# First sums over the output weights, written into the ordered part of steps 18 to 21

## The chip, the cores and the metric

The kernel runs on one core of one Trainium2 chip. The metric is device microseconds of one execution; runs are compared by their medians. Three runs of the kernel before gave 511.87 us in the median (510.62 to 513.28).

## What is computed

Two stages in one program, both in 32-bit floats. The first is attention over 4 batches, 8 heads, 768 positions and 64 numbers a head. Every position sees its neighbours closer than 16, and 24 summaries of blocks of 32 positions (the largest key of a block, the mean of its values):

```python
scores_l_m = np.where(np.abs(pos[:, None] - pos[None, :]) < 16, scale * q @ k.T, -1e9)
scores_s = scale * q @ k_sum.T + np.log(32)
a = np.exp(scores_all - max)          # scores_all: both, side by side
a = a / (a.sum(-1) + 1e-9)
x = a @ concat(v, v_sum)              # heads side by side: 3072 x 512
```

The second is a network on those 3072 rows, with weights of 512x1024, 512x1024, 1024x1024 and 1024x512:

```python
h = ((x @ w1) * (x @ w2)) @ w3
out = h @ w_out
```

## The kernel before

**Precision.** TensorE multiplies a rounded 32-bit format here, so each operand is kept as a high part and a low part (`low`, line 120: the number less its rounded copy), and each product is three matmuls. ScalarE makes the rounded copy, VectorE the subtraction.

**Stages.** `w3` and `w_out` are first multiplied with each other into eight tiles `wp` (the output weights). The first 1024 rows go through the network in the plain way. The other 2048 rows, in two units n = 1 and 2, are multiplied by a scheme with seven products of half-size blocks in place of eight. It needs sums and differences of blocks: of the rows (`xT`, `moving_x`), of the gates' weights (`sums_of_gates`, stored to the device memory `wS`) and of the output weights (`sums_of_output`, stored to `pS`). `stationary` (line 665) makes such sums: four additions on VectorE (lines 689, 691, 695, 700) on the quarters `wr`, and for each result a cast on ScalarE (line 679, into a tile `sp`), the low half on VectorE (line 121), and a write by SyncE (line 685).

**The gates' products.** For a unit, `gates` runs twice (r = 0, 1) over seven products, and each over four banks of PSUM (tiles `ln`), with six matmuls of 512 columns a bank (line 740). After every product each bank is read out by `add_up`: a copy on ScalarE (line 758) or an addition on VectorE (line 760). The next product can't write a bank before. Each product takes two weight tiles `ws` of 512 KB, one for two banks. SyncE loads them (line 785) into six slots that they share with the tiles `sp` of the gates' sums.

**Attention beside it.** Steps 0 to 23 (a unit of 512 positions by a pair of heads) are interleaved with the network; from step 16 on two at a time, in `two_steps(m)` with steps 2m and 2m + 1. Each has scores (line 376), a masked minimum (line 390), exponentials (line 404), sums inverted (lines 409 and 410), a normalization (line 414), transposes (434, read out at 442 and 444) and products with the values (457, read out at 477). `PAIRS[0]` is 8.

**Order.** TensorE and GpSimd execute in the order in which the code was written. On ScalarE and VectorE the parts under `tc.manual_schedule(engines=VECTOR)` keep their order among themselves; all else is put by a scheduler where it sees room, and SyncE's queue is set by it too. Work in `background` is handed out one piece at a time by `tend` as TensorE's columns are written; once the order is set, each engine executes its own queue strictly one after the other.

**The sums of the output weights.** High and low part of `wp` are first added in device memory (`spill_high`, `join_wp`, into `pR`). `LATER` then calls `sums_of_output(0)` in the first half of m = 8 and `sums_of_output(1)` in that of m = 9. Each loads four pieces of 256 KB into `wr` (line 957) and puts `stationary(...)` into `background`.

Of the kernel before, what the change touches and what calls it, by code (L numbers as in the profile page):

```python
# [73 lines left out]
def attention_moe(ctx, tc, qG, kW, kT, vP, vW, vB, mask, w1, w2, w3T, wo, out, outT):  # L74
    nc = tc.nc
    B, NPAIR, _, S = kT.shape
# [13 lines left out]
    NF = w1.shape[0] * FQ // P  # L90
    NJ = w3T.shape[2] // 2 // P
    DO = out.shape[1]
    NK = 7
# [18 lines left out]
    wp = [sb.tile([P, 2, DO], F32R, name=f"wp{i}", tag="wp", bufs=NF) for i in range(NF)]  # L112
# [299 lines left out]
    def normalize(sm, mx):  # L412
        for j in range(NI):
            nc.scalar.activation(sm[:, j], sm[:, j], AF.Copy, scale=mx[:, 2, j : j + 1])  # L414
# [250 lines left out]
    def stationary(name, load, to_dram, home, apart=None):  # L665


        if apart is not None:
            t = apart
        else:  # L670
            whole = sb.tile([P, 2, 2, 512], F32, name="wr", tag="ring", bufs=RING)
            t = [[whole[:, i, j] for j in range(2)] for i in range(2)]
        yield from load(t)
        (a11, a12), (a21, a22) = t
        yield 1

        def finished(k, raw):
            to = sb.tile([P, 2, 512], F32R, name="sp", **home)
            nc.scalar.copy(to[:, 0], raw)
            yield 1  # L680
            low(nc.vector, to[:, 1], raw, to[:, 0])
            yield 1
            yield 1
            yield 1
            nc.sync.dma_start(to_dram(k), to.bitcast(F32))
            stored.add((name, k))

        works = []
        nc.vector.tensor_tensor(a22, a21, a22, ALU.add)
        yield 1  # L690
        nc.vector.tensor_tensor(a21, a11, a21, ALU.subtract)
        works.append(finished(2, a22))
        next(works[0])
        yield 1
        nc.vector.tensor_tensor(a11, a22, a11, ALU.subtract)
        works.append(finished(5, a21))
        next(works[0])
        next(works[1])
        yield 1
        nc.vector.tensor_tensor(a12, a12, a11, ALU.subtract)  # L700
        if apart is not None:
            yield from staggered([*works, finished(4, a11), finished(3, a12)])
            return

        yield from staggered(works)
        for _ in range(3):
            yield 1
        yield from staggered([finished(4, a11), finished(3, a12)])
# [57 lines left out]
    def moving_x(n, at):  # L766

        o = ORDERS[n]
        k = o.ids[at]

        def start():
            while any(kept.get((n, half), 0) < NC for half in range(2 if k > 1 else 1)):
                yield -1
            t = sb.tile([P, 2, KH, U], F32R, name="xT", tag="w12", bufs=8)
            works = []
            for c in range(KH):
                b = [[raws[n, half][c + i * KH] if (n, half) in raws else None for half in range(2)] for i in range(2)]
                works.append(moving(o, k, b, (t[:, 0, c], t[:, 1, c]), o.before.get(k, (k,))))
            yield from staggered(works)
            xT[n, k] = t  # L780

        tasks.append(start())
# [161 lines left out]

        return stationary("w%d" % q, load, lambda k: wS[k][q], {"tag": "x", "bufs": 6})

    def sums_of_output(c):

        if c:
            two = [sb.tile([P, 2, 512], F32, name="wr", tag="raw", bufs=2) for _ in range(2)]  # L950
            t = [[two[i][:, j] for j in range(2)] for i in range(2)]
        else:
            t = [[sb.tile([P, 512], F32, name="wr", tag="pt", bufs=4) for _ in range(2)] for _ in range(2)]
        for h in range(2):
            for i in range(2):
                to = t[i][h].rearrange("p (j d) -> p j d", d=DH)
                nc.sync.dma_start(to, pR[c][:, h, :, i * DH : (i + 1) * DH])
        background.append(stationary("p%d" % c, lambda _: range(1, 3), lambda k: pS[k][c], {"tag": "wp", "bufs": NF}, t))

    def network():  # L960
        for u in range(2):
# [299 lines left out]
    def begins(m):  # L1261
# [6 lines left out]
        15: [lambda: flow_in(4), lambda: moving_x(1, 2)],  # L1268
    }
    LATER = {  # L1270
        (PAIRS[0], 0): [lambda: sums_of_output(0)],
        (PAIRS[0], 1): [lambda k=k: moving_x(1, k) for k in range(3, NK)],
        (PAIRS[0] + 1, 0): [lambda: sums_of_output(1)],
    }

    for i in range(NF):
# [50 lines left out]
    def two_steps(m):  # L1327

        a, b = 2 * m, 2 * m + 1
        first = m == PAIRS[0]  # L1330
        if first:
            fetch_means(*place(a - 1), values[a - 1])
        with tc.manual_schedule(engines=VECTOR):
            if first:
                t, home = sms.pop(a - 2)
                pt = evacuate(transposes(t), "A", home)
            for p in (a - 4, b - 4):
                if p in turned:
                    finish_step(p, turned.pop(p), **SPARE)
            if m in PAIRS:  # L1340
                (u, sm, mx, sc), (u2, sm2, mx2, sc2) = [begin(p) for p in (a, b)]
                reduce(u, 0, sc, sm, mx)
                expose(0, sm, mx)
                reduce(u, 1, sc, sm, mx)
        if not first:
            fetch_values(a - 2)
        for work in LATER.get((m, 0), ()):
            work()
        if m in PAIRS:
            fetch(a + 2)  # L1350
            run(given[0] + LEAD / 2)
            with tc.manual_schedule(engines=VECTOR):
                expose(1, sm, mx)
                reduce(u2, 0, sc2, sm2, mx2)
                invert(mx)
            run(given[0] + LEAD / 2)
            with tc.manual_schedule(engines=VECTOR):
                if first:
                    finish_step(a - 2, pt, **SPARE)
                    turn((a - 1,), "A")  # L1360
                expose(0, sm2, mx2)
                reduce(u2, 1, sc2, sm2, mx2)
                normalize(sm, mx)
            if not first:
                fetch_values(b - 2)
            fetch(b + 2)
            run(CLASSIC + LAST_SINGLE * FAST if first else (given[0] + begins(m + 1)) / 2)
            with tc.manual_schedule(engines=VECTOR):
                if first:
                    finish_step(a - 1, turned.pop(a - 1), **SPARE)  # L1370
                expose(1, sm2, mx2)
                invert(mx2)
                normalize(sm2, mx2)
        if not first and m - 1 <= PAIRS[-1]:
            with tc.manual_schedule(engines=VECTOR):
                turn((a - 2, b - 2), "A")
        if m not in PAIRS:
            fetch_values(b - 2)
        for p in (a, b):
            fill(p + 2)  # L1380
            if not first and p - 2 in values:
                fetch_means(*place(p - 2), values[p - 2])
        for work in LATER.get((m, 1), ()):
            work()
        run(begins(m + 1))
# [75 lines left out]
```

## Time and profile before

| | |
|---|---|
| median of three runs | 511.87 us |
| the profiled execution | 513.02 us, of which the span is 511.2 |
| TensorE busy | 487.2 us (95%) |
| VectorE, ScalarE busy | 357.7 us (70%), 317.2 us (62%) |
| mean granted TensorE clock | 0.992 |
| moved by DMA | 139.29 MB, 272 GB/s in the mean |

The span runs from the first instruction to the last. Busy shares are means over stages that have different limits. A wait is read from the engine that waits; the idle time of an engine counts only where another engine waits for it in turn. The granted clock is 1.00 at the higher of TensorE's two levels and 0.50 at the lower.

### The profile page before, as it was taken

How to read it: one execution, taken by the hardware profiler on the slowest of the kernel's cores; microseconds unless marked ns; L12 is line 12 of the kernel's file. 1: busy time of each engine (PE TensorE's matmuls, PEld its weight loads, DVE VectorE, ACT ScalarE, POOL GpSimd, SP SyncE). 2: the span in 40 equal slices, each digit the busy share in tenths (PEclk: the TensorE clock that was granted, in tenths of full speed). 3: DMA queues.
4: the chain of work that ended last, by engine and by line, in shares of the span. 5: the costliest groups of instructions: out<-in, count | busy, mean ns of one | idle time of the engine just before them, and what ended most of it. 6: DMA issues, size and time to landing. Idle time of an engine off the chain costs nothing.

```text
span 511.2 us, 10548 instructions
## 1 busy us (share of the span) xinstructions
PE 487.2 (95%) x3804; PEld 393.5 (77%) x3804; DVE 357.7 (70%) x873; ACT 317.2 (62%) x882; POOL 61.3 (12%) x121
## 2 busy tenths in 40 slices
PE   0989999999999999999977999999999999999997
PEld 0767777888877878777856888888888888888886
DVE  5969886897703879875469787579969029229972
ACT  5589864776726978877974959579734421422710
POOL 1024522000212010000210304022000000000000
PEclk9999999999999999999997999999999999999999
DMA  8998697999599998888998989995859766656752
GB/s 341 413 410 272 223 361 252 364 402 388 161 324 242 287 260 284 281 293 287 336 296 288 309 313 317 368 259 181 233 187 248 254 190 199 197 178 204 211 188 96
DMA packets 56068, 139.29 MB, mean 272 GB/s; under 512 B 6224, under 2 KB 19280, under 8 KB 53456
## 3 DMA queue, kind: packets, MB, share of 16 engines
q1 hardware_dynamic: 51600, 127.44, 73.2%
q0 software_dynamic: 3264, 9.08, 7.7%
q10 hardware_dynamic: 1152, 2.10, 1.1%
q8 instruction: 30, 0.49, 0.4%
q14 instruction: 22, 0.18, 0.1%
HBM read 105.89 MB, written 32.70 MB: 271 GB/s over the span
## 4 chain that ended last, share of the span: by engine, by line
PE 76%; ACT 8%; DMA 7%; DVE 5%; issue 1%; POOL 0%; SPq 0%; POOLq 0%; DVEq 0%; ACTq 0%
PE ln L740 42%; PE mm L125 26%; PE po L457 4%; PE sc L376 3%; DMA k<-in_kW_dram 3%; PE tp L434 2%; DMA wr<-pR 2%; ACT wf L176 2%; ACT sm L404 2%; DVE wf L206 2%; ACT w L220 1%; DVE w L121 1%; DMA wraw<-in_w_dram 1%; DVE wf L203 1%; DMA wraw<-in_wo_dram 1%
## 5 line engine op out<-in xcount | busy, mean ns | idle before, releaser
L740 PE MATMUL ln<-xT,ws 128*128 128x512 f32 x672 | 158.8, 396 | 5.7 <-DVE tmp L760 4.9
L740 PEld LDWEIGHTS ln<-xT,ws 128*128 128x128 f32 x672 | 127.2, 191 | 34.3 <-DVE tmp L760 5.3
L125 PE MATMUL mm<-x,w 128*128 128x512 f32 x384 | 90.9, 394 | 0.5 <-DVE g L531 0.5
L125 PEld LDWEIGHTS mm<-x,w 128*128 128x128 f32 x384 | 71.1, 188 | 16.9 <-DVE g L531 0.9
L404 ACT ACTIVATE sm<-sm,mx 128x120 f32<-128x120 f32 x192 | 73.8, 390 | 9.8 <-DVE mx L390 9.6
L740 PE MATMUL ln<-hT,ws 128*128 128x512 f32 (+1 forms) x348 | 77.6, 383 | 0.2 <-ACT tmp L758 0.2
L740 PEld LDWEIGHTS ln<-hT,ws 128*128 128x128 f32 x348 | 63.6, 188 | 13.3 <-ACT tmp L758 0.6
L760 DVE TENSOR_TENSOR tmp<-ln,tmp 128x512 f32<-128x512 f32 (+1 forms) x53 | 35.5, 674 | 53.8 <-PE ln L740 39.0
L125 PE MATMUL mm<-w,w 128*128 128x512 f32 x192 | 51.1, 418 | 13.7 <-ACT w L220 11.8
L643 ACT CAST hT<-hr 128x512 fp32r<-128x512 f32 x56 | 32.1, 622 | 41.8 <-DVE hr L817 33.1
L125 PEld LDWEIGHTS mm<-w,w 128*128 128x128 f32 x192 | 36.8, 197 | 24.9 <-ACT w L220 12.0
L390 DVE CUSTOM_DVE_ANT_0 sm<-sc,mask_sb 128x120 f32<-128x120 f32 x192 | 41.3, 275 | 15.7 <-PE sc L376 15.7
L125 PE MATMUL mm<-wp,h 128*128 128x512 f32 x192 | 46.3, 395 | 0.0
L414 ACT ACTIVATE sm<-sm,mx 128x120 f32<-128x120 f32 x128 | 38.8, 384 | 6.8 <-DVE mx L410 6.8
L125 PEld LDWEIGHTS mm<-wp,h 128*128 128x128 f32 x192 | 35.4, 188 | 8.4 <-issue 0.5
L121 DVE TENSOR_TENSOR hT<-hr,hT 128x512 fp32r<-128x512 f32 x56 | 35.6, 681 | 4.0 <-ACT hT L643 3.9
L404 ACT ACTIVATION_READ_ACCUMULATOR sm<-sm,mx 128x1 f32 x192 | 37.2, 194 | 0.0
L121 DVE TENSOR_TENSOR w<-wf,w 128x1024 fp32r<-128x1024 f32 (+1 forms) x22 | 25.6, 1167 | 8.2 <-ACT w L220 8.2
L220 ACT CAST w<-wf 128x1024 fp32r<-128x1024 f32 (+1 forms) x22 | 21.4, 973 | 14.6 <-DVE wf L206 13.3
L363 POOL COPY k<-ks 128x96 f32<-128x96 f32 (+1 forms) x32 | 10.1, 328 | 150.3 <-DMA k<-in_kW_dram 113.2
L176 ACT ACTIVATE wf<-wraw 128x1024 f32<-128x1024 f32 (+1 forms) x22 | 23.2, 1065 | 7.7 <-DMA wraw<-in_wo_dram 3.5
L758 ACT COPY tmp<-ln 128x512 f32<-128x512 f32 x32 | 18.8, 588 | 14.4 <-PE ln L740 13.3
(72 smaller groups left out, 569.7 us busy)
## 6 DMA issues: line engine op xcount, KB each, us to landing
ws<-wS SPq DMA_DIRECT2D x56, 512.0 KB
wraw<-in_w3T_dram SPq DMA_DIRECT2D x8, 1024.0 KB
wraw<-in_w_dram SPq DMA_DIRECT2D x8, 1024.0 KB
wS<-sp SPq DMA_DIRECT2D x16, 512.0 KB
ws<-pS SPq DMA_DIRECT2D x16, 512.0 KB
raw<-in_kT_dram SPq DMA_DIRECT2D x16, 392.0 KB
wS<-w SPq DMA_DIRECT2D x12, 512.0 KB
ws<-pW SPq DMA_DIRECT2D x24, 256.0 KB
```

What stands on the lines that cost most here:

```text
L121: eng.tensor_tensor(dst, src, hi.bitcast(F32), ALU.subtract)
L125: nc.tensor.matmul(acc, lhsT=a, rhs=b, start=first and i == 0, stop=last and i == len(terms) - 1)
L176: nc.scalar.activation(f[:, some], words[:, some, 1].bitcast(F32), AF.Prelu, scale=2.0**-112, alpha=-(2.0**32),)
L220: nc.scalar.copy(t[:, 0, some], f[:, some])
L390: nc.vector.tensor_tensor_reduce(out=sm[:, j], in0=sc[h][:, i * KR : (i + 1) * KR], in1=mask_sb[:, 0 if blk == 0 else 2 if blk == BLOCKS - ...
L404: nc.scalar.activation(sm[:, j], sm[:, j], AF.Exp, bias=mx[:, 0, j : j + 1], scale=-1.0, accum_out=mx[:, 1, j : j + 1])
L414: nc.scalar.activation(sm[:, j], sm[:, j], AF.Copy, scale=mx[:, 2, j : j + 1])
L457: nc.tensor.matmul(po[cols, at : at + 64], lhsT=v[:KR, g, i, cols], rhs=pt[g][:, (h * NBLK + i) * 64 : (h * NBLK + i + 1) * 64], start=Tru ...
L643: nc.scalar.copy(dst[0], src)
L740: nc.tensor.matmul(bank[:, cols], lhsT=x, rhs=y[:, cols], start=c + j == 0 and (split or k in o.first), stop=c == steps - 1 and j == 2 and ...
L758: nc.scalar.copy(parts[to][:, cols], got)
L760: nc.vector.tensor_tensor(parts[to][:, cols], got, parts[more][:, cols], ALU.add)
```

## The change

`sums_of_output` is split. `load_joined(c)` makes the tiles and loads them; it is called for c = 0 and 1 in the first and the second half of m = 8. The sums themselves come from a generator, of which six pieces are drawn right behind the second softmax of m = 9 (c = 0, steps 18 and 19) and m = 10 (c = 1, steps 20 and 21), inside the part whose order on ScalarE and VectorE is kept. Six pieces hold the four additions and the first casts; the rest goes to `background` as before. The two empty pieces ahead of the first addition (`range(1, 3)`) are gone.

```diff
--- before.py
+++ after.py
@@ -944,7 +944,9 @@
 
         return stationary("w%d" % q, load, lambda k: wS[k][q], {"tag": "x", "bufs": 6})
 
-    def sums_of_output(c):
+    joined = {}
+
+    def load_joined(c):
 
         if c:
             two = [sb.tile([P, 2, 512], F32, name="wr", tag="raw", bufs=2) for _ in range(2)]
@@ -955,7 +957,10 @@
             for i in range(2):
                 to = t[i][h].rearrange("p (j d) -> p j d", d=DH)
                 nc.sync.dma_start(to, pR[c][:, h, :, i * DH : (i + 1) * DH])
-        background.append(stationary("p%d" % c, lambda _: range(1, 3), lambda k: pS[k][c], {"tag": "wp", "bufs": NF}, t))
+        joined[c] = t
+
+    def sums_of_output(c):
+        return stationary("p%d" % c, lambda _: (), lambda k: pS[k][c], {"tag": "wp", "bufs": NF}, joined.pop(c))
 
     def network():
         for u in range(2):
@@ -1268,9 +1273,8 @@
         15: [lambda: flow_in(4), lambda: moving_x(1, 2)],
     }
     LATER = {
-        (PAIRS[0], 0): [lambda: sums_of_output(0)],
-        (PAIRS[0], 1): [lambda k=k: moving_x(1, k) for k in range(3, NK)],
-        (PAIRS[0] + 1, 0): [lambda: sums_of_output(1)],
+        (PAIRS[0], 0): [lambda: load_joined(0)],
+        (PAIRS[0], 1): [lambda: load_joined(1), *(lambda k=k: moving_x(1, k) for k in range(3, NK))],
     }
 
     for i in range(NF):
@@ -1371,6 +1375,11 @@
                 expose(1, sm2, mx2)
                 invert(mx2)
                 normalize(sm2, mx2)
+                if m - 1 - PAIRS[0] in joined:
+                    sums = sums_of_output(m - 1 - PAIRS[0])
+                    for _ in range(6):
+                        next(sums)
+                    background.append(sums)
         if not first and m - 1 <= PAIRS[-1]:
             with tc.manual_schedule(engines=VECTOR):
                 turn((a - 2, b - 2), "A")
```

TensorE's and GpSimd's queues hold the same rows in the same order. On SyncE the loads of `wr` stand where they stood; writes of `pS` and loads of `ws` change places from the second half of unit 1's first seven products on.

VectorE, in the first seven products of unit 1, behind the minima of step 17, before (`wr` are quarters of the output weights, `sp_3184` and `sp_3194` sums of the gates' weights, `xraw` and `xT` rows of unit 1, `mx` a softmax's sums, `ln_3172` the first bank):

```order
L689 TENSOR_TENSOR wr_3163<-wr_3162,wr_3163 128x512
L121 TENSOR_TENSOR sp_3184<-wr_3059,sp_3184 128x512
L410 RECIPROCAL mx_3108<-mx_3108 128x8
L691 TENSOR_TENSOR wr_3162<-wr_3160,wr_3162 128x512
L695 TENSOR_TENSOR wr_3160<-wr_3163,wr_3160 128x512
L639 TENSOR_TENSOR xraw_2179<-xraw_2849,xraw_2179 128x512
L121 TENSOR_TENSOR xT_3377<-xraw_2849,xT_3377 128x512
L639 TENSOR_TENSOR xraw_2849<-xraw_2849 128x512
L639 TENSOR_TENSOR xraw_2180<-xraw_2180,xraw_2179 128x512
L700 TENSOR_TENSOR wr_3161<-wr_3161,wr_3160 128x512
L121 TENSOR_TENSOR sp_3194<-wr_3059,sp_3194 128x512
L689 TENSOR_TENSOR wr_3520<-wr_3520 128x512
```

Six more rows follow before the addition that reads out `ln_3172`. And now:

```order
L121 TENSOR_TENSOR sp_3184<-wr_3059,sp_3184 128x512
L410 RECIPROCAL mx_3108<-mx_3108 128x8
L639 TENSOR_TENSOR xraw_2179<-xraw_2849,xraw_2179 128x512
L639 TENSOR_TENSOR xraw_2849<-xraw_2849 128x512
L121 TENSOR_TENSOR xT_3383<-xraw_2849,xT_3383 128x512
L639 TENSOR_TENSOR xraw_2180<-xraw_2180,xraw_2179 128x512
L121 TENSOR_TENSOR sp_3194<-wr_3059,sp_3194 128x512
L639 TENSOR_TENSOR xraw_2179<-xraw_2849,xraw_2179 128x512
L639 TENSOR_TENSOR xraw_2849<-xraw_2849 128x512
L639 TENSOR_TENSOR xraw_2180<-xraw_2180,xraw_2179 128x512
L760 TENSOR_TENSOR tmp_3190<-ln_3172,tmp_3190 128x512
```

The eight sums are gone from here, and the low half of `sp_3184` is the first row.

ScalarE, at the eighth product of unit 1 (`tmp` are the four copies that read out its banks), before:

```order
L758 COPY tmp_3777<-ln_3762 128x512
L679 CAST sp_3781<-wr_3162 128x512
L758 COPY tmp_3790<-ln_3763 128x512
L758 COPY tmp_3800<-ln_3764 128x512
L679 CAST sp_3803<-wr_3160 128x512
L758 COPY tmp_3811<-ln_3765 128x512
```

And now:

```order
L679 CAST sp_3689<-wr_3162 128x512
L679 CAST sp_3753<-wr_3160 128x512
L643 CAST hT_4274<-hr_3189 128x512
L679 CAST sp_3759<-wr_3161 128x512
L758 COPY tmp_3791<-ln_3776 128x512
L758 COPY tmp_3801<-ln_3777 128x512
L758 COPY tmp_3810<-ln_3778 128x512
L758 COPY tmp_3818<-ln_3779 128x512
```

Three casts of the first block of sums now stand ahead of the four copies; before, they stood between and behind them.

VectorE, at the tenth and eleventh product of unit 1 (`ln_3776` to `ln_3779`, `ln_3762` to `ln_3765` before, are the four banks), before:

```order
L760 TENSOR_TENSOR tmp_3800<-ln_3764,tmp_3800 128x512
L410 RECIPROCAL mx_3877<-mx_3877 128x8
L121 TENSOR_TENSOR sp_4120<-wr_3519,sp_4120 128x512
L760 TENSOR_TENSOR tmp_3811<-ln_3765,tmp_3811 128x512
L121 TENSOR_TENSOR sp_4130<-wr_3519,sp_4130 128x512
L760 TENSOR_TENSOR hr_3776<-ln_3762,tmp_3777 128x512
L760 TENSOR_TENSOR hr_3776<-ln_3763,tmp_3790 128x512
```

And now:

```order
L410 RECIPROCAL mx_3881<-mx_3881 128x8
L689 TENSOR_TENSOR wr_3360<-wr_3360 128x512
L760 TENSOR_TENSOR tmp_3810<-ln_3778,tmp_3810 128x512
L691 TENSOR_TENSOR wr_3360<-wr_3359,wr_3360 128x512
L760 TENSOR_TENSOR tmp_3818<-ln_3779,tmp_3818 128x512
L695 TENSOR_TENSOR wr_3359<-wr_3360,wr_3359 128x512
L760 TENSOR_TENSOR hr_3790<-ln_3776,tmp_3791 128x512
L121 TENSOR_TENSOR sp_4054<-wr_3360,sp_4054 128x512
L700 TENSOR_TENSOR wr_3359<-wr_3359 128x512
L121 TENSOR_TENSOR sp_4058<-wr_3360,sp_4058 128x512
L121 TENSOR_TENSOR sp_4120<-wr_3359,sp_4120 128x512
L760 TENSOR_TENSOR hr_3790<-ln_3777,tmp_3801 128x512
```

The second block's four sums and three of its low halves now stand between the additions that read out the banks, and the reciprocal stands ahead of the third bank's.

## Rows read from the trace of the kernel before

**Rows 1.** what TensorE (PE) waited for, whole run: waiter <- releaser: us, times, longest

```profile
PE ln L740 <- DVE tmp L760: 4.9, 1, 4.9
```

**Rows 2.** timeline of PE: start us, us, line, operation, idle before and its releaser

```profile
257.69 5.08 PE L740 MATMUL ln<-xT,ws 128*128 128x512 f32 x21
263.59 3.03 PE L740 MATMUL ln<-xT,ws 128*128 128x512 f32 x12 [0.83 <-ACT hr L758]
271.50 8.54 PE L740 MATMUL ln<-xT,ws 128*128 128x512 f32 x24 [4.88 <-DVE tmp L760]
...
281.77 13.26 PE L740 MATMUL ln<-xT,ws 128*128 128x512 f32 x57
```

**Rows 3.** stretches: us, PE busy (instructions), granted clock, DMA share, GB/s

```profile
269.00:270.00 1.00, 0.00 (x0) 1.00 0.89 336
270.00:271.00 1.00, 0.00 (x0) 0.84 0.98 396
...
271.50:277.00 5.50, 5.50 (x13) 0.50 0.89 300
```

**Rows 4.** timeline of VectorE (DVE) at the place

```profile
258.74 0.69 DVE L689 TENSOR_TENSOR wr<-wr 128x512 f32<-128x512 f32 x1 [10.44 <-DMA wr<-pR]
...
266.17 0.69 DVE L689 TENSOR_TENSOR wr<-wr 128x512 f32<-128x512 f32 x1 [1.13 <-DMA wr<-pR]
...
268.96 1.89 DVE L639 TENSOR_TENSOR xraw<-xraw 128x512 f32<-128x512 f32 x3
270.77 0.68 DVE L760 TENSOR_TENSOR tmp<-ln,tmp 128x512 f32<-128x512 f32 x1
```

**Rows 5.** timeline of ScalarE (ACT) at the place

```profile
251.52 0.63 ACT L679 CAST sp<-wr 128x512 fp32r<-128x512 f32 x1
...
260.18 0.40 ACT L414 ACTIVATE sm<-sm,mx 128x120 f32<-128x120 f32 x1 [2.35 <-DVE mx L410]
...
262.97 0.56 ACT L758 COPY hr<-ln 128x512 f32<-128x512 f32 x1
263.44 0.58 ACT L477 COPY xraw<-po 128x512 f32<-128x512 f32 x1
```

**Rows 6.** what SyncE's queue (SPq) waited for, 255 to 275

```profile
SPq L785 <- DMA wS<-sp: 6.4, 2, 4.1
```

**Rows 7.** timeline of SyncE's queue at the place

```profile
254.03 0.36 SPq L957 DMA_DIRECT2D wr<-pR  x1
...
255.01 0.88 SPq L957 DMA_DIRECT2D wr<-pR  x2
260.06 0.33 SPq L685 DMA_DIRECT2D wS<-sp  x1
...
264.73 0.85 SPq L785 DMA_DIRECT2D ws<-wS  x2
265.67 0.39 SPq L685 DMA_DIRECT2D wS<-sp  x1
...
271.85 0.81 SPq L785 DMA_DIRECT2D ws<-wS  x2
```

**Rows 8.** stretches with all engines: PE, PEld, DVE, ACT, POOL busy; clock, DMA share, GB/s

```profile
256.00:258.00 2.00, 2.00 (x36) 1.52 (x36) 0.00 (x0) 1.83 (x8) 1.53 (x3) 1.00 1.02 370
...
264.00:266.00 2.00, 2.00 (x10) 1.59 (x9) 1.04 (x2) 2.00 (x11) 0.00 (x0) 1.00 0.63 166
```

**Rows 9.** timeline of PE, the second quarter of the gates' products

```profile
305.15 2.09 PE L457 MATMUL po<-sm,v 120*64 120x64 f32 x64
...
309.40 12.54 PE L740 MATMUL ln<-xT,ws 128*128 128x512 f32 x54
...
322.96 8.49 PE L740 MATMUL ln<-xT,ws 128*128 128x512 f32 x36
```

**Rows 10.** timeline of DVE there

```profile
319.26 0.69 DVE L760 TENSOR_TENSOR tmp<-ln,tmp 128x512 f32<-128x512 f32 x1 [0.67 <-PE ln L740]
321.31 0.20 DVE L410 RECIPROCAL mx<-mx 128x8 f32<-128x8 f32 x1 [1.36 <-ACT mx L409]
```

## The prediction

> **What bounds the kernel now.** I read the page first, then the list of what TensorE waited for, then the timelines of TensorE, VectorE, ScalarE and SyncE around the longest wait, the table by stretch for the granted clock and the DMA share, and last the order of the instructions before and after the change.
>
> TensorE is busy for 95% of the span, so only its idle time and its slow time can be won. Beside the start of the program, nearly all of its idle time lies in one place: 4.9 us in which it waited for a VectorE addition of line 760 [rows 1]. The timeline shows the place, and 0.83 us just ahead of it for a ScalarE copy of line 758. TensorE ends the third of seven products at 266.62, stands still, and begins the fourth (24 matmuls) at 271.50 [rows 2]. These 24 take 8.54 us, where 57 of the same shape later take 13.26, or 0.233 each. So 24 should take 5.58, and 2.96 us are lost to speed. The granted clock says why: 1.00 up to 270, 0.84 in the next microsecond, and 0.50, the lower of its two levels (1.2 GHz), after the stall [rows 3]. The clock fell at the end of an idle time of 4.88 us. It had not fallen in the idle 0.83 us before. So the place costs 0.83 + 4.88 + 2.96 = 8.67 us.
>
> What VectorE did there: it stood still for 10.44 us, from 248.3 to 258.74, in front of the first sum over the output weights (line 689), whose input `wr` was still being loaded [rows 4]. Its queue runs in order. Behind that sum stood work that had long been ready: the low half of `sp_3184`, which ScalarE had prepared at 252.1, and the reciprocal, for which ScalarE then waited 2.35 us before its normalization at 260.18 [rows 5]. At 266.17 the second block of sums came, after another wait for `wr`, and then took 4 x 0.7 us; the addition that frees TensorE's bank stood behind all of it and started at 270.77.
>
> **What the change takes away there.** In the new order none of the eight sums stands between 248.3 and the freeing additions; the first pair of order pieces above shows it. ScalarE's normalization starts at about 257.8, when its exponentials end, and its copy of the third bank comes some 2.4 us earlier than 262.97, ahead of TensorE. So the 0.83 go. On VectorE three subtractions of `xraw` remain ahead of the freeing addition; they wait for ScalarE's copy at 263.44, which moves up by 2.4 us to 261.0 and ends at 261.6. Three subtractions (1.9 before) and the addition itself bring us to 264.1 [rows 4, 5]. TensorE needs it at 265.80, which is 262.77 (the end of the row at 257.69) plus 3.03 [rows 2]. VectorE is then 1.7 us early and no longer sets the time.
>
> **What is late next.** The fourth product also needs its weights, `ws_3298`. Its slot was held by `sp_3184`, so SyncE issues this load only after the write of `sp_3184` has landed: it waited for such writes 6.4 us in two waits, 4.1 the longer [rows 6]. The write stood at 260.06, since VectorE's low half came at 259.35 behind the stalled sum. Ahead of it in SyncE's queue are only two loads of `wr` at 255.01, which took 0.88. So the write can now go at 255.9, 4.2 us earlier [rows 7].
>
> How long it takes to land is not shown for that moment; two like it are. The write at 260.06 let the load go at 264.73, 4.67 us later, with the queue nearly drained: the DMA share falls to 0.63 in 264 to 266 [rows 8]. The write at 265.67, with two loads of 512 KB ahead, let the next load go at 271.85, 6.18 us later. At 255.9 the engines are fully busy (share 1.02), with three loads of `wr` and one of `ws` just issued, so the second is the nearer. I take 6.7, a little more than that: the load of `ws_3298` goes at 262.6. For the load itself the nearest row is that of `wr` issued at 254.03, for which VectorE started at 258.74: 4.71 us. So the weights are there at 267.3, and TensorE starts its fourth product at 267.4, after 1.6 us of waiting.
>
> Bounds of this term: 255.9 + 4.67 + 4.71 = 265.3, earlier than needed (no wait); and a load that goes no earlier than before, 264.73 + 4.71 = 269.4 (3.6 us of waiting). An idle time of 1.6 us lies between the 0.83 that left the clock alone and the 4.88 that did not; in that stall the row of 269 to 270 still reads 1.00 [rows 3]. I take it that it stays.
>
> The Trainium skill, DMA: Bandwidth & Descriptors, section "Anatomy of one DMA — SWDGE (gpsimd) path", gives a transfer a fixed cost of some 2 us plus its bytes over 436 GB/s, for the path that GpSimd issues. For 512 KB this would be an estimate of 3.2 us, by which there would be no wait at all; the rows of SyncE's writes are 1.5 to 3 us above it, so I go by the rows.
>
> **What it adds later.** Nothing is new: the eight sums of 0.6 to 0.7 us, their casts and their writes move some 25 to 50 us later; the eight loads of `wr` keep their places on SyncE, GpSimd's queue is the same row for row. TensorE's order is the same too.
>
> First block: on ScalarE the cast of `sp_3759` waits for VectorE's last sum and now stands ahead of the four copies that free the banks of the next product (second order piece). Behind these banks TensorE has 4.2 us of other work, from 305.15 to 309.40, before it needs the first of them again [rows 9]; the sums that the cast waits for end by my count 1.5 us before the fourth of these banks is full. I cost it at nothing. Without that cover the four copies would come about 2 us late.
>
> Second block: VectorE did the third bank's addition at 319.26 and the reciprocal, which waits for ScalarE, at 321.31 [rows 10]. Now the reciprocal and the first sum stand ahead of that addition (third order piece), so it ends near 322.7. TensorE needs this bank at 324.4: 322.96 plus six matmuls of 0.236 [rows 9]. Four operations later the tightest is the addition of the second bank, by the same count done at 327.6 to 328.1 and needed at 328.6. So 0.5 to 1.6 us of cover; if it is gone, TensorE waits a microsecond or two there. The writes of the eight `sp` tiles now stand ahead of weight loads that are used over 10 us later by the same count. I cost this at nothing too.
>
> **The sum.** The fourth product starts at 267.4 in place of 271.50: 4.1 us, which holds the 0.83 and 3.3 of the 4.88. The clock gives 2.96. Together 7.1 us. All later stretches have TensorE back to back, so the end moves with it. The profiled execution took 513.02 (its span of 511.2 and 1.8 around it): 505.9. The median of the runs shown is 511.87, 1.15 below it, so I forecast 504.8.
>
> **Rivals.**
> - The weights come in time and the place vanishes entirely: 8.67 us, 503.2. For it: the faster of the two writes measured, with which the load is there at 265.3. The Trainium skill's fixed cost above (DMA: Bandwidth & Descriptors) speaks for it as well. Against: the DMA engines are fully busy there.
> - The load hardly moves: the write queues behind the other loads until about when it landed before, TensorE starts at 269.4, 2.1 us are won, and the clock falls as it did: 509.8 (506.8 if the clock holds). For it: in a full queue the total of bytes ahead stays the same, wherever the write stands.
> - Nothing is won: the sums leave the place, as the order shows, but the wait only changes hands, from VectorE to the weights' load, landing at 271.5 or so. That would be 511.9. Against: the load would have to take 7 us from its issue of before.
> - Slower: the second block. If the casts and the reciprocal reach VectorE late, the eight instructions between the freeing additions hold all four banks, and TensorE stands for about the length of that block, 8 x 0.68 = 5.4 us, plus the clock's 2.96. It would decide only if the weights' load had eaten the gain as well (the case before): 511.9 + 8.4 = 520. It begins to cost where the second bank's addition is over 0.5 us later than I count.
>
> **How the numbers follow.** The forecast 0.55; place gone entirely 0.20; load hardly earlier 0.12; nothing won 0.07; slower 0.06. About 0.5% (2.6 us) is what a measurement of this kernel can tell from no change. The forecast, the first rival and half of the second are faster by more: 0.81. The other half and the third are within it: 0.13. Slower: 0.06. The range goes from 502.0, the first rival less the 1.2 us by which the fastest run shown lies below the median, to 510.0, which takes in the second rival at the lower clock; beyond it lie the last two rivals, 0.13.
>
> **What would show it.** VectorE no longer idle for 10 us after 248.3; the write of `sp_3184` issued near 255.9 and the first two loads after it at 261 to 264; TensorE's wait ahead of the fourth product between nothing and 3 us, ended by the DMA of `ws` and not by line 760; the granted clock at 1.00 through it; no new wait in the next 60 us. A wait on line 760 or 758 ahead of the products after that, or a clock of 0.50 after the load's wait, would prove me wrong.

## The result and the profile after

The changed kernel takes 508.87 us (median of 22 runs, 503.81 to 512.8); the kernel before, beside it, took 511.78 (22 runs). The ratio is 0.9917, with a 95% interval of 0.9892 to 0.9942: 0.8% faster. The ratio leaves out three slow runs of the changed kernel, 511.74 to 512.8 us. The forecast was 504.8 in a range of 502.0 to 510.0. So the direction is as foretold, and of the 7.1 us forecast 2.9 came by the medians (4.36 by the two profiled executions: 513.02 and 508.66, span 506.9).

In the list of what TensorE waited for, line 760 is gone [rows 1]; a load of weights stands there in its place (waiter <- releaser: us in total, times, longest):

```profile
PE ln L740 <- DMA ws<-wS: 3.2, 1, 3.2
```

The timeline of TensorE (start us, us, engine, line, operation, idle before and its releaser) shows the place that answers to [rows 2]:

```profile
258.12 7.78 PE L740 MATMUL ln<-xT,ws 128*128 128x512 f32 x33
269.05 5.72 PE L740 MATMUL ln<-xT,ws 128*128 128x512 f32 x24 [3.15 <-DMA ws<-wS]
...
276.50 13.26 PE L740 MATMUL ln<-xT,ws 128*128 128x512 f32 x57
```

The 0.83 us for ScalarE are gone (33 matmuls run in one piece to 265.90; the row of 57 at 276.50 is the undisturbed pace). The wait is 3.15 in place of 4.88, and the 24 matmuls behind it take 5.72 in place of 8.54. The stretches (us, busy time of PE, PEld, DVE, ACT and POOL, granted clock, DMA share, GB/s) say why, against [rows 3]: the clock did not fall in this execution.

```profile
265.90:269.05 3.15, 0.00 (x0) 0.03 (x1) 2.50 (x5) 3.15 (x11) 0.00 (x0) 1.00 0.97 262
269.05:271.00 1.95, 1.95 (x9) 1.60 (x10) 0.29 (x1) 0.47 (x1) 0.00 (x0) 1.00 0.95 357
```

So the place costs 3.15 us of wait and 0.14 of slower pace (5.72 less 5.58), 3.29 in place of 8.67: 5.4 won. About 1.1 of it is lost elsewhere: the third product begins 0.43 later than in the profile before, and there are two short waits of the scores, 0.22 at 303.17 and 0.60 at 330.43, for which no row gives a releaser. (At the first of them the kernel before lost some 0.4 as well: its 64 scores took 2.31 us there, against 1.87 elsewhere.)

VectorE does what was foretold: it no longer stands for 10.44 us [rows 4], and line 760 begins at 263.34 (264.1 by the forecast). From its timeline:

```profile
252.13 0.69 DVE L121 TENSOR_TENSOR sp<-wr,sp 128x512 fp32r<-128x512 f32 x1 [3.67 <-ACT sp L679]
...
261.53 1.90 DVE L639 TENSOR_TENSOR xraw<-xraw 128x512 f32<-128x512 f32 x3 [4.64 <-ACT xraw L477]
263.34 0.68 DVE L760 TENSOR_TENSOR tmp<-ln,tmp 128x512 f32<-128x512 f32 x1
```

SyncE's timeline is where the rest went. It answers to [rows 7]:

```profile
253.50 0.89 SPq L959 DMA_DIRECT2D wr<-pR  x2
254.71 0.33 SPq L685 DMA_DIRECT2D wS<-sp  x1
256.20 0.98 SPq L959 DMA_DIRECT2D wr<-pR  x2
258.17 0.32 SPq L359 DMA_DIRECT2D v<-vS  x1
264.95 0.88 SPq L785 DMA_DIRECT2D ws<-wS  x2
```

The write of `sp_3184` goes at 254.71, 5.35 us earlier than before, and the load of `ws_3298` that waits for it goes at 264.95, where before it went at 264.73. The list of SyncE's waits, against [rows 6], has the write as releaser:

```profile
SPq L785 <- DMA wS<-sp: 9.3, 2, 6.1
```

The write takes 10.24 us from issue to release, where the forecast had 6.7. This is the mechanism of the second rival, "the load hardly moves", to which I gave 0.12. Its numbers (TensorE starts at 269.4; 509.8 us, or 506.8 if the clock holds) stand near the measured 269.05 and 508.87.

The clock is a second difference between runs. Of the 19 runs that the ratio rests on, nine had a mean granted clock of 0.999 or 1.000 (median 505.5 us) and ten one of 0.995 to 0.997 (median 509.4). The profile above is of the first kind; experiments 7 and 8 show the second.

### The profile page after: what moved, and what is told of

Same layout as the page of the kernel before. It is cut to its first block, busy times and chain, and to the rows that moved or that the text cites. A ratio compares the mean times of both kernels' runs of the same rounds, so it can differ in the third digit from the quotient of the medians.

```text
span 506.9 us, 10543 instructions
## 1 busy us (share of the span) xinstructions
PE 483.1 (95%) x3804; PEld 391.0 (77%) x3804; DVE 357.0 (70%) x873; ACT 316.6 (62%) x882; POOL 66.5 (13%) x121
## 4 chain that ended last, share of the span: by engine, by line
PE 73%; DMA 13%; DVE 6%; ACT 5%; issue 1%; SPq 1%; POOL 0%; POOLq 0%; DVEq 0%; ACTq 0%
PE ln L740 39%; PE mm L125 25%; PE sc L376 4%; PE po L457 3%; DMA k<-in_kW_dram 3%; DMA ws<-wS 3%; DMA v<-in_vW_dram 2%; DMA wS<-sp 2%; PE tp L434 2%; ACT sm L404 2%; DVE w L121 2%; DVE wf L206 1%; DMA vS<-vs 1%; DMA wraw<-in_w_dram 1%; ACT w L220 1%; DMA wraw<-in_wo_dram 1%
## 5 line engine op out<-in xcount | busy, mean ns | idle before, releaser
L740 PE MATMUL ln<-xT,ws 128*128 128x512 f32 x672 | 155.6, 391 | 3.2 <-DMA ws<-wS 3.2
L740 PEld LDWEIGHTS ln<-xT,ws 128*128 128x128 f32 x672 | 125.4, 188 | 30.4 <-DVE xT L121 3.5
L125 PE MATMUL mm<-w,w 128*128 128x512 f32 x192 | 49.9, 409 | 15.1 <-ACT w L220 12.5
L363 POOL COPY k<-ks 128x96 f32<-128x96 f32 (+1 forms) x32 | 14.8, 476 | 157.0 <-DMA k<-in_kW_dram 140.6
L376 PE MATMUL sc<-k,q 64*64 64x120 f32 x768 | 25.4, 268 | 1.6 <-issue 0.8
```

What stands on the lines that cost most here:

```text
L125: nc.tensor.matmul(acc, lhsT=a, rhs=b, start=first and i == 0, stop=last and i == len(terms) - 1)
L376: nc.tensor.matmul(sc[h][64 * g : 64 * g + 64, i * KR : (i + 1) * KR], lhsT=q[rows, i * P + 64 * g : i * P + 64 * g + 64], rhs=k[rows, i, ...
L740: nc.tensor.matmul(bank[:, cols], lhsT=x, rhs=y[:, cols], start=c + j == 0 and (split or k in o.first), stop=c == steps - 1 and j == 2 and ...
```

## The experiments

**Theories.** A: what is left of the place is a chain, the write of `sp_3184` and, only when it has landed, the load of `ws_3298` into the same buffer; the write lands late because of the bytes queued with it. B: bandwidth alone; the weights would come as late by any route. C: such a write takes its 10 us by itself. D: this wait matters little. Each time below is beside the kernel before on the same chip.

**1. The chain cut.** The two sums get buffers of another tag, so the load finds a free buffer.

```
-            to = sb.tile([P, 2, 512], F32R, name="sp", **home)
+            to = sb.tile([P, 2, 512], F32R, name="sp", **(home(k) if callable(home) else home))
...
-        return stationary("w%d" % q, load, lambda k: wS[k][q], {"tag": "x", "bufs": 6})
+        return stationary("w%d" % q, load, lambda k: wS[k][q], lambda k: {"tag": "wp", "bufs": NF} if q == 3 and k in (2, 5) else {"tag": "x", "bufs": 6})
```

> The two sums sp_3184 and sp_3194 of the gates' weights get buffers of the tag 'wp' in place of the tag 'x', so the load of ws_3298 takes a buffer that is free and no longer waits for the write of sp_3184; SyncE issues write, load, write, load, and then the four loads of wr of c=1. Theory A (the wait of 3.15 us is the chain: write of sp_3184 lands after 10.2 us, and only then the load of 4.0 us is issued): the load is issued near 255 in place of 264.95, is there by 265 to 266, TensorE's wait ahead of the fourth product falls from 3.15 us to under 0.7, the granted clock stays at 1.00 in all runs, and the time goes from 508.9 to 503.5-505. Rival B (bandwidth alone: the same bytes stand ahead of the weights by any route): the load lands near 268.9 again, the wait stays 2.5 to 3.2 us, and the time stays at 508-509. Rival D (the gain of 2.9 is eaten at another place, and this wait matters little): the wait goes and the time moves by less than 1.5 us.

Measured: 504.99 us against 512.26, ratio 0.986 (0.9826 to 0.9894); clock 0.998 to 1.000 in all six runs. The timeline of SyncE has the load 0.6 us behind the write, and that of TensorE has third and fourth product in one piece, 57 matmuls without a wait:

```profile
249.90 0.57 SPq L685 DMA_DIRECT2D wS<-sp  x1
250.52 0.44 SPq L785 DMA_DIRECT2D ws<-wS  x1
```

```profile
256.87 13.21 PE L740 MATMUL ln<-xT,ws 128*128 128x512 f32 x57
270.01 1.87 PE L376 MATMUL sc<-k,q 64*64 64x120 f32 x64
```

A holds; D falls, and B with it. The edit did one thing more: SyncE now issues the four loads of `wr` of c=1 behind both pairs of write and load (from 254.15), where in the changed kernel two of them stood ahead of the write. Those 512 KB are an estimated 1.4 us at the 375 GB/s of these stretches, and the wait that went was 3.15; experiment 4 keeps the two causes apart. This version beats both kernels by its median; its interval touches that of the changed kernel, and the two were not run side by side.

**2. and 3. Fewer bytes around the write, chain kept.** The loads of `wr` of c=1 (then of both halves) are held back by one-element copies that need the reciprocal of step 19.

```
+        if c in TIED:
+            with tc.manual_schedule(engines=VECTOR):
+                for i in range(2):
+                    for h in range(2):
+                        nc.vector.tensor_copy(t[i][h][:1, :1], tied[0][:1, 2, :1])
...
                 invert(mx2)
+                tied.append(mx2)
...
+    TIED, tied = (1,), []
```

In the third kernel `TIED` is (0, 1), and the call of `load_joined(0)` stands beside that of c=1.

> The loads of wr for c=1 (four of 256 KB) wait for the reciprocal of step 19 (265.25 in the changed kernel), by four copies of one element on VectorE; so 512 KB fewer stand ahead of the write of sp_3184 on SyncE, and 512 KB fewer right behind it. The slot chain stays. Theory A with a write that is slow by the bytes queued ahead of it: it lands 1.4 us earlier (512 KB at 0.375 MB/us), near 263.5, and near 262 if the bytes behind it compete as well; the wait ahead of the fourth product falls from 3.15 to 0.2-1.7 us; the clock stays up in more of the runs; 505 to 507.5. Rival C (such a write takes its 10 us whatever else is queued): it lands 10 us after its issue near 253.7, at 263.7-264, wait 2.0-2.5 us, 507-508.5. Rival D: less than 1.5 us of change at any length of the wait.

> As the run before, and the four loads of wr for c=0 wait for the same reciprocal too: 1 MB more is gone from the queue ahead of the write of sp_3184. The slot chain stays. Theory A with the bytes ahead: the write takes some 5 us in place of 10.2, lands by 258.5-260, the load of ws_3298 is there by 264, no wait is left, the clock stays at 1.00 in all runs, 503.5 to 505. Rival C (10 us in any queue): issued near 253, lands at 263, wait about 1.2 us, and the DMA share stays below 1 meanwhile; 505.5-507. Beside both: the eight loads now start near 266 and compete with the weights of the products after the fourth (issued 267.40 to 277); if those come late, a new wait ended by the DMA of ws stands at 281 to 305 and eats part of it.

Measured: c=1 alone 507.71 against 512.26, ratio 0.9898 (0.9855 to 0.994); both halves 511.59, ratio 0.9958 (0.992 to 0.9996). SyncE's timelines, c=1 first, then both:

```profile
252.29 0.42 SPq L685 DMA_DIRECT2D wS<-sp  x1
252.75 3.50 SPq L359 DMA_DIRECT2D v<-vS  x4
261.29 0.34 SPq L785 DMA_DIRECT2D ws<-wS  x1
```

```profile
255.08 0.32 SPq L685 DMA_DIRECT2D wS<-sp  x1
255.50 2.04 SPq L359 DMA_DIRECT2D v<-vS  x4
259.07 0.34 SPq L785 DMA_DIRECT2D ws<-wS  x1
```

The write takes 9.00 us with 512 KB less ahead of it (and 512 KB less behind it), and 3.99 with 1.5 MB less ahead (5.90 and 5.71 in the two later executions). C falls. The wait ahead of the fourth product was 0.92 us and then none. But the time did not follow: the loads that were held back now stand ahead of later weights. With c=1 held back, the timeline of TensorE has a wait of 2.65 us at 315.81 for `ws`, behind which the clock read 0.83 in 310 to 320. With both, the profile had no such wait, while eight of twelve runs had a clock of 0.992 or 0.993; so the same kernel was profiled twice more. (The 509.47 us of that first profile come from other places: a wait of 2.24 us for line 531 at 91, ahead of anything that this edit touches, and one of 1.46 inside the scores at 331.)

> The kernel with all eight loads of wr tied to the reciprocal of step 19 again: its profile showed no wait ahead of the fourth product and yet the median of its runs is 511.6, at a clock of 0.993 in most. Theory: in most runs the eight loads (2 MB), now issued from 268.9 in one piece ahead of five loads of weights, make a later product wait for its weights by 3 to 5 us, between 285 and 320, and the clock falls there. Rival: the fall is at another place, as at 91 us, where the profile had 2.24 us of wait for VectorE and a clock of 0.83 in 90 to 100.

> The kernel with all eight loads of wr tied to the reciprocal of step 19 a third time; the two executions profiled had no wait ahead of the fourth product, and 8 of 12 timed ones a clock of 0.992 or 0.993. If the late loads are the cost, a wait of 3 us or more ended by the DMA of ws or of wr, or by line 760, stands between 280 and 320, and the clock falls behind it.

The first of the two (505.93 us, clock 1.000) had a wait of 1.53 us for line 760 at 282.49, and one of 0.90 inside the scores. The second (511.46, clock 0.993) showed the cost, in TensorE's timeline:

```profile
257.43 13.21 PE L740 MATMUL ln<-xT,ws 128*128 128x512 f32 x57
...
285.92 7.91 PE L740 MATMUL ln<-xT,ws 128*128 128x512 f32 x21 [5.05 <-DMA ws<-wS]
```

and in its stretches the clock falling ahead of that product:

```profile
282.00:285.92 3.92, 0.00 (x1) 0.03 (x1) 1.44 (x3) 2.53 (x8) 0.00 (x0) 0.91 1.01 379
285.92:290.00 4.08, 4.08 (x10) 3.21 (x11) 1.15 (x2) 0.00 (x0) 0.27 (x1) 0.50 0.80 319
```

That is 5.05 us of wait, and 2.9 more for 21 matmuls that take 5.05 at full speed: in this execution the wait moved from 266 to 281.

**4. Both edits.** Own buffers, and c=1 held back.

> Both edits: own buffers for sp_3184 and sp_3194, and the loads of wr for c=1 tied to the reciprocal of step 19. Theory A: as with own buffers alone there is no wait left to win ahead of the fourth product, so the time is that of own buffers alone within 1 us (503.5 to 505), with the load of ws_3298 landing earlier still. Rival B (bandwidth): this one is faster than own buffers alone by 1.5 us or more, since 1 MB stands behind the weights in place of ahead.

Measured: 505.79, ratio 0.9891 (0.9843 to 0.994), within 1 us of own buffers alone, as A has it. Beside experiment 2, where the same loads were held back and the chain stood, only the buffers differ: the wait ahead of the fourth product goes from 0.92 us to none, and the time from 507.71 to 505.79, a step within the intervals of the two. So with those loads out of the way the chain is worth some 0.9 us of wait; how much of the 3.15 it is worth with them in the queue was not measured by itself. The profile has a wait of 2.91 us at 317.89 for line 760 that own buffers alone don't have. On VectorE the reciprocal, which waited 2.29 us for ScalarE, and two sums of the second block stood ahead of that addition, so here the second block cost what the prediction put at nothing.

**5. and 6. One half of the change at a time.** In the first, c=1 goes back to the background work (without the two empty pieces that stood ahead of its sums before), in the second, c=0.

```
-        (PAIRS[0], 1): [lambda: load_joined(1), *(lambda k=k: moving_x(1, k) for k in range(3, NK))],
+        (PAIRS[0], 1): [lambda k=k: moving_x(1, k) for k in range(3, NK)],
+        (PAIRS[0] + 1, 0): [lambda: load_joined(1), lambda: background.append(sums_of_output(1))],
```

```
-        (PAIRS[0], 0): [lambda: load_joined(0)],
+        (PAIRS[0], 0): [lambda: load_joined(0), lambda: background.append(sums_of_output(0))],
```

> Only the four first sums of the first half (c=0) stand at their new place; those of c=1 are written where they were. Theory A (two waits stand at this place one behind the other: VectorE's addition of line 760 and the load of ws_3298, and the second alone decides in the changed kernel): the write of sp_3184 goes as in the changed kernel near 254.7 and the load near 265, there at 269; but VectorE has the four sums of c=1 ahead of line 760 and waits for their wr until 264-266, so line 760 starts near 269.5-270.5, TensorE's wait is 4 us, ended by VectorE, and the clock falls in most runs; 509.5 to 512. Rival E (the 10 us stand of VectorE in front of c=0 was the whole cost): as the changed kernel, 508-509.

> Only the four first sums of c=1 stand at their new place; VectorE still stands for some 10 us in front of the first sum of c=0. Theory A with a write that lands by when the queue drains and not by when it is issued: the write goes near 260, 5 us later than in the changed kernel, lands near 264.7 all the same, the load is there near 269; line 760 starts near 267, ahead of it. So the fourth product starts at 269, with the same wait ended by the DMA of ws, and the time is that of the changed kernel, 508 to 510. Rival E (the early write is what won): the load goes later by some microseconds, fourth product after 270.5, 510.5 to 512.

Measured: c=0 alone 517.28 against 512.05, ratio 1.0105 (1.0058 to 1.0153): slower. c=1 alone 507.23, ratio 0.99 (0.9868 to 0.9933): the whole gain of the change. SyncE's timelines, c=0 alone first:

```profile
254.24 0.33 SPq L685 DMA_DIRECT2D wS<-sp  x1
255.46 1.02 SPq L959 DMA_DIRECT2D wr<-pR  x2
257.48 0.32 SPq L359 DMA_DIRECT2D v<-vS  x1
264.00 0.81 SPq L785 DMA_DIRECT2D ws<-wS  x2
```

```profile
259.82 0.33 SPq L685 DMA_DIRECT2D wS<-sp  x1
260.26 1.30 SPq L959 DMA_DIRECT2D wr<-pR  x2
261.66 0.49 SPq L359 DMA_DIRECT2D v<-vS  x1
264.03 0.82 SPq L785 DMA_DIRECT2D ws<-wS  x2
```

This pair is the clearest reading of the study. The instructions of SyncE are in the same order, the write is issued 5.58 us apart, and the load behind it goes 0.03 us apart. In the second kernel VectorE still stands for 9.20 us in front of c=0, and it costs nothing there: line 760 begins at 266.53 and ends at 267.21, 0.5 us before TensorE starts, and TensorE's wait of 1.26 us is for `ws`. Theory A as refined in that expectation holds, and rival E falls in both.

I had not expected that c=0 alone would be slower than before. Its place at 266 is as foretold (line 760 at 270.05, 4.74 us of wait). The rest is a second wait, in the timelines of TensorE and then of ScalarE:

```profile
308.23 8.51 PE L740 MATMUL ln<-xT,ws 128*128 128x512 f32 x36
319.65 1.70 PE L740 MATMUL ln<-xT,ws 128*128 128x512 f32 x6 [2.91 <-ACT hr L758]
322.26 5.49 PE L740 MATMUL ln<-xT,ws 128*128 128x512 f32 x12 [0.91 <-ACT hr L758]
```

```profile
318.12 0.62 ACT L679 CAST sp<-wr 128x512 fp32r<-128x512 f32 x1 [3.10 <-DMA pS<-sp]
319.03 0.56 ACT L758 COPY hr<-ln 128x512 f32<-128x512 f32 x1
```

Of the casts of the two halves the last two need buffers whose writes have not landed; the copy that frees TensorE's bank stands behind them on ScalarE. The clock read 0.50 behind these two waits too (322.3 to 324). That is close to the fourth rival (sums that hold the banks of the second quarter), with ScalarE in VectorE's role. In the changed kernel, where the first sums of the two halves begin at 286.24 and 316.21, there is no such wait.

**7. and 8. The changed kernel again.**

> The changed kernel again, for the length of the wait ahead of the fourth product and for the clock there. If the wait is the chain write then load, it is 2.5 to 5 us in every execution and ended by the DMA of ws; where it is long, the granted clock falls to 0.50 behind it, which would be the lower clock of 13 of the 22 timed runs. If the clock falls elsewhere, some other place costs time in those runs.

> The changed kernel a third time: from the write of sp_3184 to the issue of ws_3298 9.7 to 10.3 us as in the two executions before it, a wait of 2.5 to 3.5 us ahead of the fourth product, and either the clock holds (time lost there about 3) or it falls to 0.50 behind the wait (about 4.5 to 6).

Measured: 509.54 us at a clock of 0.997, and 513.42 at 0.993. The intervals from write to load were 9.75 and 8.93 us (the second under the 9.7 that I expected), the waits 2.70 and 3.41. TensorE's timelines, one execution after the other:

```profile
268.79 7.36 PE L740 MATMUL ln<-xT,ws 128*128 128x512 f32 x24 [2.70 <-DVE xT L121]
```

```profile
269.47 7.32 PE L740 MATMUL ln<-xT,ws 128*128 128x512 f32 x24 [3.41 <-DMA ws<-wS]
...
330.59 1.25 PE L376 MATMUL sc<-k,q 64*64 64x120 f32 x38
333.58 0.98 PE L376 MATMUL sc<-k,q 64*64 64x120 f32 x26 [1.74 <-issue]
334.48 10.75 PE L740 MATMUL ln<-xT,ws 128*128 128x512 f32 x39
```

In the first of them a subtraction of VectorE that ended at 268.66 is named; the load of `ws_3298`, issued at 265.07, takes 3.7 to 4.1 us in the other executions of these kernels and so would be there at 268.8 or a little later. The two ended close together, and which came last is open. In both executions the clock fell behind the wait: the stretch of 271 to 272 of the first reads

```profile
271.00:272.00 1.00, 1.00 (x4) 0.73 (x3) 0.75 (x2) 0.00 (x0) 0.00 (x0) 0.50 1.01 406
```

So 24 matmuls took 7.3 us in place of 5.58. The second execution has one more wait, 1.74 us in the middle of the 64 scores, and the clock falls there again (39 matmuls in 10.75, where they take 9.13 in the first). The same instruction waited 0.60 in the changed kernel's first profile and not at all in the first execution here. No row names a releaser; what the DMA records say of it stands further down.

**9. The chain cut in the kernel before.** The edit of experiment 1, sums not moved.

> The kernel before, sums where they were, with only the buffers of sp_3184 and sp_3194 changed to the tag 'wp'. SyncE then issues write, load of ws_3298, write, load ahead of the loads of wr for c=1; with those later, the sums of c=1 come behind line 760 on VectorE by themselves, while VectorE still stands in front of the first sum of c=0 until its wr is there. Theory A (the landing of write and then load in a full queue is what is worth winning; VectorE's own wait for wr of c=0 ends early enough, as it did with only c=1 moved, where line 760 began at 266.5): the load lands by 266, line 760 starts at 264.5-266.5, wait ahead of the fourth product under 1 us, clock up, 504.5 to 507. Rival E (the sums of c=0 have to leave for the gain): line 760 starts after 268, wait of 2.5 us or more, 508.5 to 512.

Measured: 508.56 against 511.25, ratio 0.9953 (0.993 to 0.9975). The mechanism is as A has it: no wait for `ws`, line 760 at 264.09, clock 0.999 or 1.000 in eleven of twelve runs. The size is not: 2.7 us won in place of some 4 to 7. TensorE's timeline shows small waits for VectorE. Sums of c=1 now fall between the additions, and the first of them (line 689 at 269.29) had itself waited 1.46 us for its `wr`:

```profile
257.43 12.12 PE L740 MATMUL ln<-xT,ws 128*128 128x512 f32 x51
270.64 1.66 PE L740 MATMUL ln<-xT,ws 128*128 128x512 f32 x6 [1.09 <-DVE tmp L760]
...
274.03 14.08 PE L740 MATMUL ln<-xT,ws 128*128 128x512 f32 x57
```

They are 1.09, 0.67 at 294.90, and 0.8 in a row of 57 that takes 13.26 undisturbed. So the moved sums alone are worth 2.9 us, the own buffers alone (with the order on SyncE that comes with them) 2.7, and both together 7.3.

**10. Loads ahead of the weights.** Own buffers, and all eight loads of `wr` issued early.

```
-        (PAIRS[0], 0): [lambda: load_joined(0)],
-        (PAIRS[0], 1): [lambda: load_joined(1), *(lambda k=k: moving_x(1, k) for k in range(3, NK))],
+        (PAIRS[0], 0): [lambda: load_joined(0), lambda: load_joined(1)],
+        (PAIRS[0], 1): [*(lambda k=k: moving_x(1, k) for k in range(3, NK))],
```

> As with own buffers for sp_3184 and sp_3194, but all eight loads of wr (2 MB) are issued ahead of the weights of the third and fourth product. Theory A with landing by the bytes queued ahead: the fourth product's weights come no later than 267 (one passage through the queue), but those of the third product (needed at 258) now stand behind 1 MB more, 2.7 us at 0.375 MB/us: a wait of 0 to 3 us ended by the DMA of ws ahead of the third product, at 245 to 258, takes the place of the one at 266; 505 to 508.5. Rival F (loads issued ahead do not delay those behind, as long as no slot is waited for): no wait at either place, 503.5 to 505, as with own buffers alone.

Measured: 508.78 against 511.25, ratio 0.9953 (0.9928 to 0.9978). TensorE's timeline has the wait inside the third product:

```profile
257.23 2.33 PE L740 MATMUL ln<-xT,ws 128*128 128x512 f32 x9
263.62 13.93 PE L740 MATMUL ln<-xT,ws 128*128 128x512 f32 x48 [4.05 <-DMA ws<-wS]
```

4.05 us, more than the 3 that I allowed, and a lower clock behind it (0.50 in 263.62 to 266). Bytes ahead delay those behind with no buffer waited for: F falls.

## Why the forecast was right in sign and too large

**What came as foretold.** The 0.83 us for ScalarE gone; VectorE ahead of TensorE (line 760 at 263.34); the write issued early (254.71 against 255.9); the load itself (4.1 us from issue to the fourth product against 4.71); the wait handed to the load of `ws_3298`. Of the second half of the text, no cost came at the two later blocks: the additions around them had no wait of TensorE behind them.

**The step that failed** is "I take 6.7, a little more than that: the load of `ws_3298` goes at 262.6". The interval was 10.24 us, in two further executions 9.75 and 8.93. I had two rows of such writes, 4.67 and 6.18, and read them as a time that a write takes. The runs show them as what was left of the queue when the write was issued:

| kernel | write issued | load issued | between |
|---|---|---|---|
| before | 260.06 | 264.73 | 4.67 |
| c=1 alone moved | 259.82 | 264.03 | 4.21 |
| c=0 alone moved | 254.24 | 264.00 | 9.76 |
| changed | 254.71 | 264.95 | 10.24 |
| changed, `wr` of c=1 held back | 252.29 | 261.29 | 9.00 |
| changed, all `wr` held back | 255.08 | 259.07 | 3.99 |

With the same loads on SyncE the moment of landing is the same, whether the write went at 254 or at 260. In each of these six executions the DMA share is near 1 while the write is out and falls to 0.7 or less within a microsecond or two of the load's issue. I had called the 4.67 a time "with the queue nearly drained", by the 0.63 of 264 to 266 [rows 8]; that is the share when the write landed. While it was out, the stretches of the kernel before read 1.01 and 1.00:

```profile
260.00:262.00 2.00, 2.00 (x11) 1.57 (x10) 1.97 (x6) 1.82 (x6) 0.00 (x0) 1.00 1.01 283
262.00:264.00 2.00, 1.17 (x6) 0.66 (x5) 2.00 (x5) 2.00 (x7) 0.00 (x0) 1.00 1.00 308
```

Which bytes the write stood behind no row shows. So to let the write go earlier won nothing, and the stand of VectorE in front of c=0, on which most of my reading dwelt, was hidden behind the queue. What the change won, it won by taking c=1's four sums from in front of line 760. The second rival said just this ("in a full queue the total of bytes ahead stays the same, wherever the write stands"), and the rows of a DMA share of 1.02 [rows 8] were cited for the choice of a slow write; they should have decided for the rival.

The Trainium skill, DMA: Bandwidth & Descriptors, section "Queues, rings and completion order", says that each DMA engine takes the descriptors of one ring in order. The table fits that (3.99 us with all `wr` held back, 10.24 with them in the queue), but no run here shows the order itself. The Trainium skill, the same page, section "Anatomy of one DMA — SWDGE (gpsimd) path", gives a fixed cost plus bytes for a DMA that GpSimd issues, an estimate of 3.2 us for such a write. All six of SyncE's writes in the table took longer, the nearest 3.99 us.

**The second term, the clock.** "I take it that it stays" held in the profiled run and failed in both further executions (waits of 2.70 and 3.41), each time for some 1.75 us. Worked out for the place, the three executions of the changed kernel cost 3.29, 4.48 and 5.15 us there, against 8.67: 5.4, 4.2 and 3.5 won, 4.4 in the mean. The median gain is 2.9. Part of the 1.5 between is the wait inside the scores near 331 (0.60, none, and 1.74 with a lower clock behind it). The profile gives no releaser for it, but its DMA records point at one. In the four of the fourteen profiled executions that have this wait (0.60 and 1.74 us in the changed kernel, 0.90 and 1.46 with all `wr` held back), a packet of 16 KB on q8, a queue that the profile lists as `instruction`, ended 1.0 to 1.5 us before the wait did, and the packet before it some 21 us earlier. In the ten executions without the wait that packet was through 6 to 9 us before TensorE came to the place. So a late fetch of instructions is the likely releaser. The profile does not say that q8 is TensorE's, and no experiment moved the fetch, so this is argued and not shown. The Trainium skill, Runtime: NRT & Kernel Launch, section "Instruction fetch mechanics", has each engine fetch its instructions by a DMA queue of its own. That fits, and no run here shows it.

**The chance.** What happened is in the main the second rival, at 0.12, and not the forecast, at 0.55. That 508.87 lies in the range is owed to that rival, for which the range went up to 510.0. There was luck in the sum as well: the write's term was 3.5 us too small, but the write went 1.2 us earlier than I took and the load took 0.6 less, so TensorE started only 1.65 us later than forecast. The first rival, with the place gone entirely, is reached only with the chain cut (7.3 us won, against 8.67).

## What to carry to other kernels

A transfer's time from issue to landing, read from a trace, belongs to the queue as it was then; before moving an issue earlier, add up what stands ahead of it and ask when that is through, because in a full queue the landing may not move at all. Where a load waits for a write because both use one buffer, it passes through that queue after the write has: here a buffer of its own was worth more than an earlier write. Holding back other loads can move the wait to the next weights (5.05 us in one of three executions here), and a burst of sums through few buffers can make the engine that casts them wait for its own writes to land.

## What was not expected of the hardware

TensorE's granted clock does not follow from the length of the wait alone: it held through 3.15 us in one execution of the changed kernel and through 2.91 in the kernel of experiment 4, and it fell to 0.50 (1.2 of 2.4 GHz) behind 2.65, 2.70 and 3.41 in others, and behind all the waits of 4.05 to 5.05 us seen. Waits of 1.09, 1.26 and 1.53 left it at 1.00; one of 1.74 did not. So in these executions a wait of some 1.7 to 3.5 us cost once to nearly twice its length, and two executions of one kernel differ by it.
